# Sliding-window attention scores as 64x64 tiles of the array, in a fused attention, expert and feed-forward kernel

## Chip, cores and metric

One NeuronCore of one Trainium2 chip runs the whole program. The metric is the device time of one execution in microseconds (us); the kernel before took 451.86 us, the median of three runs (451.54, 451.86 and 454.5).

## What is computed

Three blocks in a row, all in float32. Only the first one is changed.

```python
# attention: batch 2, heads 8, sequence 576, head dimension 64
scores = scale * np.matmul(q, k.transpose(0, 1, 3, 2))
rel = pos[:, None] - pos[None, :]
mask = (rel >= 0) & (rel < 64)
scores = np.where(mask, scores, -1000000000.0)
attn = np.exp(scores - max); attn = attn / (sum(attn) + 1e-09)
x = np.matmul(attn, v)            # -> 1152 tokens x 512
# mixture of 8 experts (512 -> 1024 -> 512), each token to its best expert
expert_idx = np.argmax(x @ w_gate, axis=1)
out[i] = gate_w[i] * y[expert_idx[i], pos[i]]
# dense feed-forward 512 -> 2048 -> 512 with h * relu6(h + 3) / 6
```

Each query sees itself and the 63 keys before it, so 64 queries need a window of 128 keys.

## The kernel before

**Tiling.** The 1152 tokens are nine blocks of 128, j = 0 to 8; each block is two groups of 64 queries, g = 2j and 2j + 1 (18 groups). The eight heads are four pairs hp; a pair's two heads lie on partitions 0 to 63 (even head) and 64 to 127 (odd head) after the transposes of q and k.

**A block's steps** are named nodes of a list (lines 659 to 708):

- `lq`, `lk`, `lv` load 128 rows each by DMA from SP's queue; `tq`, `tk`, `tv` (`turn_rows`, L506) transpose them on TensorE (PE), four 128x128 transposes each;
- `eq` (`q_out`, L460 on VectorE or L464 on ScalarE) copies the queries out of PSUM, scaled, into `qd`, a tile of 128 x 4 x 2 x 128. Per pair and group it is block-diagonal: the even head's 64 queries in columns 0 to 63 of partitions 0 to 63, the odd head's in columns 64 to 127 of partitions 64 to 127, and zeros elsewhere. The zeros are written once, by memsets (L376, L377), for the four buffers. So `eq` is two copies of 64 x 512;
- `ek` (L462 or L458) copies the keys into `kT`, `ev` the values into `vT`; `gw`, `ew`, `tw`, `ex` (L541, L555) bring the gate's logits through the same attention, as eight more columns of the values;
- `s` (`scores`, L570) is, per group, one 128x128 matmul per head pair: the block-diagonal queries are the stationary operand, the window of 128 keys of `kT` the moving one. The result has 128 rows, even head's queries above odd head's, in one PSUM bank. There are two banks for scores (0 and 1), taken in turn, one group each;
- `m` (`mask_max`, L583, VectorE) adds the mask and finds the row maximum, four instructions per group; `e` (`exps`, L596, ScalarE) four exponentials; `pt` (L606, PE) four transposes; `ep` (L458 or L462) the copy to `pT`;
- `av` (`values`, L624, PE) is 16 matmuls of 128 x 64 x 73 per block, for the two groups, into alternating column halves of the array; `f` (`finish`, L636 to L652, VectorE) divides and gives logits; `st` stores the rows to `x_dram`.

**What orders them.** `run_nodes` is a list scheduler that runs when the program is built: of the nodes whose needs are met it takes the one with the smallest key (estimated start, a priority from `PRIO`, its cost), and appends its instructions to the queue of PE, VectorE (DVE), ScalarE (ACT), GpSimd (POOL) or SP. For a copy it also chooses the engine, ACT or DVE. Each engine then runs its queue strictly in order. `rings` holds how many buffers of each kind there are; for a node with `take`, a buffer is reserved.

**Routing among the attention.** After five blocks (`f` of j = 4) the logits of 640 tokens are known: `top` (`choose`), `pp`, `pl`, `fl`, `gE`, `ix`, `ie` pick the fullest expert and 128 of its tokens on DVE with small matmuls between; `ga` (POOL, L799) gathers their rows from `x_dram`; `sE` (L460) scales them, and the first products with that expert's weights (`early`) fill PE while the last blocks finish. After `f` of j = 8 come the ranks of the experts (`rk`) and the slots (`sa` to `g0`), then the expert stage, whose weights (64 loads of 512 KB) come from DRAM, and from about 244 us the dense stage.

## Time and profile before

| | |
|---|---|
| median of three runs | 451.86 us |
| the profiled execution's own time | 452.26 us |
| its span, first to last instruction | 450.5 us |
| PE busy | 417.8 us, 93% |
| DVE busy | 323.6 us, 72% |
| ACT busy | 231.4 us, 51% |
| first matmul of scores | 9.54 us |
| last division of the attention (`f` of j = 8) begins | 67.48 us |

The profile is of one execution. The page gives busy times over the whole span; what one stage is limited by is read from windows of it and from timelines, which list instructions in order of their start, with the idle time before one and what ended it in brackets. A matmul's end is modelled and matmuls overlap, so on PE the distance from one start to the next tells what an instruction occupies, not its duration. A float32 matmul is two rows of the trace, a transpose one.

### The profile page before, as it was taken

The numbers are of one execution on the slowest core, as the hardware profiler recorded it, in microseconds if no ns is written. First come the engines' busy times: TensorE is split into PE (matmuls) and PEld (weight loads), VectorE is DVE, ScalarE is ACT, GpSimd is POOL, SyncE is SP. The second block draws the span as 40 slices with busy tenths as digits, with TensorE's granted clock in tenths as the row PEclk, the third lists the DMA queues.
The fourth block names the chain that finished last, engine by engine and source line by source line (L and its number), as shares of the span: only waits on it lengthen the run. The fifth ranks groups of instructions, "written<-read, shape, count | busy, mean of one in ns | idle before, by whom it ended". The sixth has DMA issues, their size and how long they took to land. (4 is left out here: it accounts for less than half of the span.)

```text
span 450.5 us, 8296 instructions
## 1 busy us (share of the span) xinstructions
PE 417.8 (93%) x2911; PEld 358.3 (80%) x2911; DVE 323.6 (72%) x861; ACT 231.4 (51%) x509; POOL 53.3 (12%) x108
## 2 busy tenths in 40 slices
PE   7999898699999899998893999999999999999994
PEld 4889775488788798986693989888888888898993
DVE  1787977679899899989552899999999722322431
ACT  3979863573567976535461744345554222422240
POOL 8624312310002002000000000000000000020011
PEclk9999999999999999999696999999999999999999
DMA  8988884997999899399774134243421000010011
GB/s 144 162 196 191 244 285 147 357 323 248 378 371 355 276 323 308 113 296 336 263 260 155 48 93 113 79 137 95 114 77 44 1 1 0 25 71 0 25 48 47
DMA packets 69651, 75.98 MB, mean 169 GB/s; under 512 B 31105, under 2 KB 49537, under 8 KB 69601
## 3 DMA queue, kind: packets, MB, share of 16 engines
q1 hardware_dynamic: 68016, 70.28, 51.3%
q0 software_dynamic: 1584, 5.08, 3.1%
q8 instruction: 25, 0.41, 0.4%
q14 instruction: 26, 0.20, 0.1%
HBM read 67.49 MB, written 7.86 MB: 167 GB/s over the span
## 5 line engine op out<-in xcount | busy, mean ns | idle before, releaser
L253 PE MATMUL banks<-x,wt 128*128 128x320 f32 (+3 forms) x576 | 108.0, 339 | 7.8 <-DVEq L1878 7.8
L253 PEld LDWEIGHTS banks<-x,wt 128*128 128x128 f32 x576 | 95.8, 191 | 17.5 <-ACT wt L267 8.0
L272 DVE TENSOR_TENSOR wt<-raw,wt 128x512 fp32r<-128x512 f32 x128 | 82.6, 685 | 18.6 <-ACT wt L267 11.3
L253 PE MATMUL banks<-wt,g 128*128 128x512 f32 x384 | 92.8, 390 | 0.0
L267 ACT CAST wt<-raw 128x512 fp32r<-128x512 f32 x128 | 74.9, 622 | 27.0 <-DMA raw<-in_moe_w_dram 14.3
L253 PEld LDWEIGHTS banks<-wt,g 128*128 128x128 f32 x384 | 71.6, 188 | 14.2
L1550 ACT ACTIVATE r<-banks,c_three 128x320 f32<-128x320 f32 (+3 forms) x48 | 27.9, 581 | 70.6 <-PE banks L253 70.6
L1553 DVE SCALAR_TENSOR_TENSOR gf<-r,banks 128x320 f32<-128x320 f32 (+3 forms) x48 | 26.6, 554 | 50.6 <-ACT r L1550 50.3
L253 PE MATMUL banks<-xT,wt 128*128 128x256 f32 (+2 forms) x288 | 40.2, 287 | 3.8 <-ACT wt L267 3.4
L253 PEld LDWEIGHTS banks<-xT,wt 128*128 128x128 f32 x288 | 35.8, 194 | 6.6 <-ACT wt L267 4.5
L253 PE MATMUL banks<-h,wt 128*128 128x256 f32 (+2 forms) x288 | 37.0, 279 | 0.0
L253 PEld LDWEIGHTS banks<-h,wt 128*128 128x128 f32 x288 | 34.6, 192 | 0.5 <-issue 0.5
L1556 ACT CAST g<-gf 128x320 fp32r<-128x320 f32 (+2 forms) x40 | 21.4, 536 | 21.8 <-DVE gf L1553 21.7
L1596 POOL DMA_INDIRECT out_dram<-raw,cidx x4 | 3.9, 982 | 225.0 <-DVE raw L1590 216.8
L1559 DVE TENSOR_TENSOR g<-gf,g 128x320 fp32r<-128x320 f32 (+2 forms) x40 | 23.3, 582 | 8.9 <-ACT g L1556 8.8
L206 ACT ACTIVATE c<-raw 128x512 f32<-128x512 f32 x32 | 21.5, 675 | 13.0 <-DVE t L230 10.4
L253 PE MATMUL banks<-wt,xT 128*128 128x256 f32 x144 | 23.0, 296 | 2.8 <-DVE wt L272 1.6
L253 PEld LDWEIGHTS banks<-wt,xT 128*128 128x128 f32 x144 | 18.9, 189 | 6.6 <-DVE wt L272 3.6
L799 POOL DMA_INDIRECT xg<-x_dram,sidx x10 | 13.9, 1388 | 84.3 <-DVE c L210 38.0
L583 DVE CUSTOM_DVE_ANT_0 neg<-banks,mask 128x128 f32<-128x128 f32 x72 | 16.5, 285 | 10.1 <-PE banks L570 10.1
L596 ACT ACTIVATE pe<-neg,nmx 128x128 f32<-128x128 f32 x72 | 22.8, 393 | 0.7 <-DVE nmx L583 0.5
L253 PE MATMUL banks<-wt,h 128*128 128x512 f32 x72 | 20.6, 423 | 2.1 <-ACT h L1430 2.1
(285 smaller groups left out, 598.9 us busy)
## 6 DMA issues: line engine op xcount, KB each, us to landing
raw<-in_moe_w_dram SPq DMA_DIRECT2D x64, 512.0 KB, 6.7
raw<-in_moe_w_in_dram SPq DMA_DIRECT2D x16, 512.0 KB, 6.0
raw<-in_moe_w_out_dram SPq DMA_DIRECT2D x16, 512.0 KB, 6.1
early<-in_moe_w_dram SPq DMA_DIRECT2D x8, 512.0 KB
wd_dram<-t SPq DMA_DIRECT2D x12, 256.0 KB, 8.1
raw<-wd_dram SPq DMA_DIRECT2D x6, 512.0 KB
x_dram<-xt SPq DMA_DIRECT2D x9, 256.0 KB, 2.4
q_sb<-in_q_dram SPq DMA_DIRECT2D x8, 256.0 KB, 5.3
```

The lines of the kernel that those rows point to most:

```text
L206: nc.scalar.activation(box["c"].bitcast(F32), box["hi"].bitcast(F32), AF.Abs)
L253: nc.tensor.matmul(out, l, r, start=(start and n == 0), stop=(stop and n == len(pairs) - 1))
L267: nc.scalar.copy(hi, r)
L272: V.tensor_tensor(out=lo, in0=r, in1=hi.bitcast(F32), op=ALU.subtract)
L583: V.tensor_tensor_reduce(out=neg[:, hp, :], in0=box["sp", g][:, hp, :], in1=mask[:, g % 2, first, :], scale=-1.0, scalar=3.0e38, op0=ALU.a ...
L596: nc.scalar.activation(pe[:, hp, :], neg[:, hp, :], AF.Exp, bias=nmx[:, hp : hp + 1], scale=-1.0)
L799: nc.gpsimd.indirect_dma_start(out=t, out_offset=None, in_=x_dram[0:n], in_offset=bass.IndirectOffsetOnAxis(ap=index.bitcast(U32), axis=0),)
L1550: nc.scalar.activation(r, ph, AF.Relu, bias=c_three)
L1553: V.scalar_tensor_tensor(out=gf, in0=r, scalar=6.0, in1=ph, op0=ALU.min, op1=ALU.mult)
L1556: nc.scalar.copy(hi, gf)
L1559: V.tensor_tensor(out=lo, in0=gf, in1=hi.bitcast(F32), op=ALU.subtract)
L1596: nc.gpsimd.indirect_dma_start(out=out, out_offset=bass.IndirectOffsetOnAxis(ap=cidx[:, a : a + 1].bitcast(U32), axis=0), in_=o, in_offset ...
```

## The change

Queries are stored without zeros, 128 x 4 x 128, by one copy of 128 x 512, and the eight memsets are gone. One node `s` now computes both groups of a block: for each head pair four products of 64 x 64 x 128, one for each half of the partitions (r: even or odd head) and each group (i). The even heads' results go to one bank, the odd heads' to the other; within a bank, group 2j stands in the upper 64 rows and group 2j + 1 in the lower. So `mask_max` of the first bank (still called g = 2j) now works on all even heads of both groups and that of the second on the odd ones; both need a mask of their own (`tmask`, six GpSimd copies), and `values` picks its rows accordingly. Both banks are one ring entry (`sp`, one buffer), free again when both `mask_max` are done. The scheduler is told new costs, so it makes a new order of the attention.

```diff
+        tmask = ac.tile([128, 3, 128], F32, name="tmask")
+        for i in range(2):
+            r = slice(64 * i, 64 * i + 64)
+            nc.gpsimd.tensor_copy(tmask[r, 0], mask[r, i, 0])
+            nc.gpsimd.tensor_copy(tmask[r, 1], mask[r, i, 1 - i])
+            nc.gpsimd.tensor_copy(tmask[r, 2], mask[r, i, i])
...
-            t = ac.tile([128, H // 2, 2, 128], F32, name=f"qd{i}")
-            eng = nc.gpsimd if i else nc.vector
-            eng.memset(t[0:64, :, :, 64:128], 0.0)
-            eng.memset(t[64:128, :, :, 0:64], 0.0)
-            qd.append(t)
+            qd.append(ac.tile([128, H // 2, 128], F32, name=f"qd{i}"))
...
-                pt, dst = box["tq", j], qd[j % NQD]
-                for s in range(2):
-                    copy(
-                        e, dst[64 * s : 64 * s + 64, :, :, 64 * s : 64 * s + 64],
-                        pt[64 * s : 64 * s + 64].rearrange("p a (n t) -> p a n t", t=64), D ** -0.5,
-                    )
+                copy(e, qd[j % NQD], box["tq", j], D ** -0.5)
...
-        def scores(g):
+        def scores(j):
             def run(e):
-                box["sp", g] = sp = quarters(bank("s"))
-                j, i = divmod(g, 2)
+                box["sp", 2 * j], box["sp", 2 * j + 1] = sp = [quarters(bank("s")) for _ in range(2)]
                 for hp in range(H // 2):
-                    nc.tensor.matmul(
-                        sp[:, hp, :], qd[j % NQD][:, hp, i, :], k_window(hp, g),
-                        start=True, stop=True,
-                    )
+                    for r in range(2):
+                        for i in range(2):
+                            d, t = slice(64 * r, 64 * r + 64), slice(64 * i, 64 * i + 64)
+                            nc.tensor.matmul(
+                                sp[r][t, hp, :], qd[j % NQD][d, hp, t], k_window(hp, 2 * j + i)[d], start=True, stop=True
+                            )
...
-                first = 1 if g % GB == 0 else 0
+                j = g // 2
+                first = [2 * j % GB, (2 * j + 1) % GB].index(0) + 1 if 0 in (2 * j % GB, (2 * j + 1) % GB) else 0
...
-                        out=neg[:, hp, :], in0=box["sp", g][:, hp, :], in1=mask[:, g % 2, first, :], scale=-1.0,
+                        out=neg[:, hp, :], in0=box["sp", g][:, hp, :], in1=tmask[:, first, :], scale=-1.0,
...
-                            box["pT", 2 * j + s][:, h // 2, 64 * (h % 2) : 64 * (h % 2) + 64],
+                            box["pT", 2 * j + h % 2][:, h // 2, 64 * s : 64 * s + 64],
...
-            node(("eq", j), p + PRIO["eq"], {"A": 0.97, "V": 1.2}, q_out(j), [("tq", j)], "qd", [("t", ("tq", j))])
+            node(("eq", j), p + PRIO["eq"], {"A": 0.5, "V": 0.6}, q_out(j), [("tq", j)], "qd", [("t", ("tq", j))])
...
-                node(("s", g), o + PRIO["s"], {"PE": 0.87}, scores(g), needs, "s", [("qd", ("eq", j))] * (g % 2))
-                node(("m", g), o + PRIO["m"], {"V": 0.84}, mask_max(g), [("s", g)], "neg", [("s", ("s", g))])
+                if g % 2 == 0:
+                    needs = [("eq", j), ("ek", j)] + [("ek", j - 1)] * (j > 0)
+                    node(("s", j), o + PRIO["s"], {"PE": 0.93}, scores(j), needs, "sp", [("qd", ("eq", j))])
+                    holders["sp", ("s", j)] = 2
+                node(("m", g), o + PRIO["m"], {"V": 0.84}, mask_max(g), [("s", j)], "neg", [("sp", ("s", j))])
```

The new order differs in the attention alone; from the division of the last block on, every engine's instructions stand as before. Two places of it. First, PE at the start: the queue from the first scores to the second transposes of probabilities (L606 before, L610 after; L570 and L574 are the scores, L541 and L540 the gate's products, L506 and L510 transposes of q, k or v, L555 and L554 the gate's small transpose). Before:

```order
L570 MATMUL banks<-kT,qd_171 128x128 x4
L541 MATMUL banks<-vT,wgb 32x128 x4
L506 MATMUL banks<-ident,q_sb 128x128 x4
L555 MATMUL banks<-ident,vw 128x128
L570 MATMUL banks<-kT,qd_171 128x128 x4
L506 MATMUL banks<-ident,k_sb 128x128 x4
L606 MATMUL banks<-ident,pe 128x128 x4
L506 MATMUL banks<-ident,v_sb 128x128 x4
L570 MATMUL banks<-kT,qd_174 128x128 x4
```

And after:

```order
L574 MATMUL banks<-kT,qd_178 64x128 x16
L540 MATMUL banks<-vT,wgb 32x128 x4
L510 MATMUL banks<-ident,q_sb 128x128 x4
L554 MATMUL banks<-ident,vw 128x128
L510 MATMUL banks<-ident,k_sb 128x128 x4
L610 MATMUL banks<-ident,pe 128x128 x4
L510 MATMUL banks<-ident,v_sb 128x128 x4
L574 MATMUL banks<-kT,qd_179 64x128 x16
L610 MATMUL banks<-ident,pe 128x128 x4
```

The second group's scores no longer stand between the first group's scores and the transposes of its probabilities.

Second, DVE near the end of the attention: the last instruction of the second-to-last `mask_max` (L583, L587), the scaling of the gathered rows (`c`, L460, L464) and the copy of their transposes (`early`). Before, both last `mask_max` stand ahead of the scaling:

```order
L583 ISA neg,nmx<-banks,mask 128x128
L583 ISA nmx 128x1
L460 TENSOR_SCALAR c_1147<-c_1147,sgE 128x512
L458 COPY early<-banks 128x512
L636 TENSOR_SCALAR rd<-banks 128x8
```

After (of the last `mask_max`, the first of its four pairs of rows):

```order
L587 ISA neg,nmx<-banks,tmask 128x128
L587 ISA nmx 128x1
L464 TENSOR_SCALAR c_1188<-c_1188,sgE 128x512
L587 ISA neg,nmx<-banks,tmask 128x128
L587 ISA nmx 128x1
```

The scaling, which waits for the gather's DMA, has moved ahead of the last block's second `mask_max`.

## Rows read from the trace of the kernel before

**Rows 1.** Windows: length, busy (count) of PE, PEld, DVE, ACT, POOL; PE clock, DMA, GB/s
```profile
9.54:42.62 33.08, 33.08 (x411) 29.16 (x412) 25.48 (x128) 27.39 (x80) 14.58 (x42) 1.00 0.89 186
42.62:64.00 21.38, 19.27 (x251) 17.15 (x251) 19.13 (x128) 17.88 (x52) 6.78 (x12) 1.00 0.88 268
64.00:67.48 3.48, 3.35 (x47) 2.70 (x46) 1.97 (x7) 1.08 (x3) 0.00 (x0) 1.00 0.45 172
```

**Rows 2.** Timeline of PE, 20 to 27 us: start, duration, instruction
```profile
20.94 1.06 PE L570 MATMUL banks<-kT,qd 128*128 128x128 f32 x8
21.84 0.60 PE L606 MATMUL banks<-ident,pe 128*128 128x128 f32 x4
...
25.16 0.60 PE L506 MATMUL banks<-ident,v_sb 128*128 128x128 f32 x4
25.60 1.06 PE L570 MATMUL banks<-kT,qd 128*128 128x128 f32 x8
26.58 0.42 PE L541 MATMUL banks<-vT,wgb 128*32 128x128 f32 x8
26.94 0.66 PE L506 MATMUL banks<-ident,q_sb 128*128 128x128 f32 x4
```

**Rows 3.** Timeline of PE: products with the values, two column halves
```profile
23.79 0.23 PE L624 MATMUL banks<-vy,pT 128*64 128x73 f32 x1
23.80 0.23 PE L624 MATMUL banks<-vx,pT 128*64 128x73 f32 x1
23.86 0.23 PE L624 MATMUL banks<-vy,pT 128*64 128x73 f32 x1
```

**Rows 4.** Groups of instructions, 0 to 100 us: copies of queries and others
```profile
L464 ACT ACTIVATE qd<-banks 64x512 f32<-64x512 f32 x14 | 8.3, 592 | 5.9 <-PE banks L506 5.8
L462 ACT COPY pT<-banks 128x512 f32<-128x512 f32 x13 | 7.5, 585 | 3.9 <-PE banks L606 3.7
L458 DVE COPY pT<-banks 128x512 f32<-128x512 f32 x5 | 3.4, 689 | 0.7 <-PE banks L606 0.7
L460 DVE TENSOR_SCALAR qd<-banks 64x512 f32<-64x512 f32 x4 | 2.8, 689 | 0.0
```

**Rows 5.** Timeline of DVE, 42 to 68 us
```profile
42.62 0.17 DVE L636 TENSOR_SCALAR rd<-banks 128x8 f32<-128x8 f32 x1 [0.28 <-PE banks L624]
...
44.09 0.20 DVE L125 TENSOR_REDUCE top_m<-logits 128x5 f32<-128x40 f32 x1
...
55.63 0.28 DVE L583 CUSTOM_DVE_ANT_0 neg<-banks,mask 128x128 f32<-128x128 f32 x1
...
56.47 0.15 DVE L792 CAST eI<-banks 128x1 int32<-128x1 f32 x1
...
56.72 0.16 DVE L794 SCALAR_TENSOR_TENSOR sgE<-banks,sgE 128x1 f32<-128x1 f32 x1
...
62.95 0.48 DVE L460 TENSOR_SCALAR c<-c,sgE 128x512 f32<-128x512 f32 x1 [0.58 <-DMA c<-x_dram,eI]
...
67.48 0.17 DVE L636 TENSOR_SCALAR rd<-banks 128x8 f32<-128x8 f32 x1 [1.26 <-PE banks L624]
```

**Rows 6.** Timeline of ACT, the last two groups' exponentials
```profile
61.56 2.44 ACT L596 ACTIVATE pe<-neg,nmx 128x128 f32<-128x128 f32 x8
```

**Rows 7.** Timelines of the start: DVE, PE, ACT
```profile
1.13 0.48 DVE L376 MEMSET qd<- 64x512 f32 x1
...
2.35 0.27 DVE L660 MEMSET warm<- 128x256 uint32 x1
...
2.67 4.02 PE L663 MATMUL banks<-warm 128*128 128x512 bf16 x9 [2.67 <-DVE warm L660]
6.49 1.06 PE L506 MATMUL banks<-ident,q_sb 128*128 128x128 f32 x4
7.49 1.12 PE L506 MATMUL banks<-ident,k_sb 128*128 128x128 f32 x4
...
7.58 1.20 ACT L464 ACTIVATE qd<-banks 64x512 f32<-64x512 f32 x2 [5.48 <-PE banks L506]
```

More of the change, by code (lines that the diff above doesn't have):

```diff
@@ L398, in tile_kernel @@
         nodes, done, emitted = {}, {}, []
-        rings = {'q': 3, 'k': 4, 'v': 3, 'qd': NQD, 't': 2, 's': 2, 'p': 1, 'o': 1, 'x': 1, 'neg': 4, 'pe': 3, 'pT': 4, 'vT': 3, 'vw': 4, 'xt': 4}
+        rings = {'q': 3, 'k': 4, 'v': 3, 'qd': NQD, 't': 2, 's': 2, 'sp': 1, 'p': 1, 'o': 1, 'x': 1, 'neg': 4, 'pe': 3, 'pT': 4, 'vT': 3, 'vw': 4, 'xt': 4}
         taken = {r: [] for r in rings}
@@ L691, in tile_kernel @@
                 o = p + g % 2
-                needs = [("eq", j), ("ek", j)] + [("ek", j - 1)] * (j > 0)
-                node(("s", g), o + PRIO["s"], {"PE": 0.87}, scores(g), needs, "s", [("qd", ("eq", j))] * (g % 2))
-                node(("m", g), o + PRIO["m"], {"V": 0.84}, mask_max(g), [("s", g)], "neg", [("s", ("s", g))])
+                if g % 2 == 0:
[3 more added lines that the diff above has]
+                node(("m", g), o + PRIO["m"], {"V": 0.84}, mask_max(g), [("s", j)], "neg", [("sp", ("s", j))])
                 node(("e", g), o + PRIO["e"], {"A": 1.17}, exps(g), [("m", g)], "pe", [("neg", ("m", g))])
```

## The prediction

> **What bounds the kernel now.** I read the page first, for where each stage lies, then windows of the attention, then the timelines of PE, DVE and ACT one beside the other, and last the list of what PE and DVE waited for. The windows [rows 1] split the attention in two. From the first scores (9.54 us) to the division of the fifth block (42.62) PE is busy for 33.08 of 33.08 us and no wait of it is listed: PE is the bound, and DVE (25.48) and ACT (27.39) have air. From 42.62 to 64.00 PE has 2.1 us of idle time, and DVE is the dense one: it gets the division of block 4, the choice of the early expert, its flags and its gates (44.09 to 56.88) besides the masks of the last blocks. Between 42.62 and 57.7 the only idle time of DVE is the 0.28 us ahead of the first row [rows 5]. So the second part is bound by DVE, and its end by a gather: the scaling of the gathered rows starts at 62.95, after 0.58 us of waiting for the DMA. The attention ends with the last division at 67.48. Behind it the change leaves every engine's order alone, and the expert stage starts from what that division gives; a shift of 67.48 is a shift of the end. So the question is only how far 67.48 moves.
>
> **Part 1, the scores on PE.** Before, a group's four products occupy 0.90 us from start to start (20.94 to 21.84), 0.98 where the next instruction has another tile shape (25.60 to 26.58) [rows 2]; 18 groups make 16.2 to 17.6 us. After, a block has 16 products of 64x64, each of which streams the same 128 columns as one product of before. Four at a time this costs 0.90 us per block, and with a change of tile shape on both sides about 0.1 more: 1.0 us. Nine blocks make 9.0, so PE loses 7.2 to 8.6 us, about 8. Does the chip run four at a time? The trace shows products side by side in column parts: the two halves for the values start 0.01 us apart and the next pair 0.06 later [rows 3], and the gate's four products, each 128 columns, take 0.36 us together (26.58 to 26.94), where one after another at 0.225 each they would take 0.90 [rows 2]. It shows no product on half of the partitions, so whether the row halves also overlap is open. Bounds: 0.9 us per block (all four together), 1.8 (column pairs together, row halves in turn: no gain), 3.6 (one after another: 16 times 0.225). I take 1.0, since both shapes with column parts overlap, and keep 1.8 and 3.6 for the rivals.
>
> The Trainium skill, "TensorE: Matmul & The Clock Gate" (Part 3, measured speedup), says that products on distinct row groups run at the same time too and gives 3.07 times for four of them. By an estimate from that page, 3.6 / 3.07 makes 1.2 us per block. The skill's "TensorEngine Tiling (Array Packing)" (Key Properties) adds that changing the tiling mode drains the engine; the 0.08 us between 0.90 and 0.98 agrees with a small price of this kind.
>
> **Part 2, the copies of the queries.** A copy of 64 x 512 takes 592 ns on ACT and 689 on DVE; copies of 128 x 512 of another tile take 585 and 689 [rows 4]. So half the partitions cost as much as all, and nine blocks lose nine copies: 18 were 8.3 + 2.8 = 11.1 us, nine are 5.3 to 6.2. But the new order puts six of the nine on DVE (before, two blocks' worth) and three on ACT. With the other copies that changed sides, DVE does 27.1 us ahead of the division of block 4, from 25.48 (the queries +1.4, one group's masks more +0.8, gate copies +1.5, keys and values -2.1); ACT loses about 4.3 in the whole attention. The saving lands on the engine that needs it less.
>
> **Part 3, the start.** The first transposes follow the nine warm-up products, which wait for a memset behind the two query memsets on DVE [rows 7]. Without these the warm-up starts 1.2 us earlier and ends near 5.3; then the transposes wait for the queries' DMA instead, which the trace bounds only by its 3.5 to 5.3 us to landing. The second transposes still start near 7.5 with their own load and need 1.0 us; the copy of the queries is 0.6 shorter, but the keys' copy follows the keys' transposes, not it. I take the first scores 0.2 us earlier, at 9.35. These first transposes take 1.0 us for four, against 0.44 later (25.16 to 25.60 [rows 2]), so PE ran at its lower level, 1.2 GHz, up to there; an earlier warm-up could end that earlier or a pause in it later, so the bounds are 0.8 us earlier and 1.0 later. On GpSimd six mask copies stand where six memsets stood, and nothing waits for them before the first masks at 10.8.
>
> **Part 4, the first half.** Up to the division of block 4 PE had 11 groups of scores; now it has six blocks of them (12 groups), and one more transpose of values: 33.08 - 11 x 0.93 + 6 x 1.0 + 0.44 = 29.3 us, from 9.35 to 38.65. DVE alone, 27.1 us from the first masks at 10.55, would end at 37.7. Two engines that both have work for 27 to 29 us and hand it to each other do not both stay full. I followed the new order row by row with the durations above (masks 0.84 per group, from 55.63 to 56.47 [rows 5]; exponentials 0.305 each, 2.44 for eight [rows 6]) and found four places where PE stands: 0.7 us before the first transposes of probabilities, since the second group's scores no longer cover the masks and exponentials of the first; 0.4 and 0.8 at the gate's products of blocks 4 and 5, whose values ACT copies behind two groups of exponentials; and 0.4 at the values of block 4, behind masks and a copy on DVE. Together 2.3, so the division of block 4 starts at about 40.9, not 42.62: of 3.8 us that PE saved so far, 1.7 arrive. Bounds: 38.9 with no wait at all, 42.6 with twice as much.
>
> **Part 5, the second half.** DVE's chain from there to the end of the early index (before: 42.62 to 56.88, 14.26 us) has the same divisions, choice, flags and gates; it loses a group of masks, a copy of probabilities and three gate copies (2.0 us), gains a copy of keys (0.6), and waits about 0.8 for the values of block 5, whose copy of probabilities stands on ACT behind the exponentials of the choice, a copy of queries and the gate copies. That is 13.6, so the index is there at 54.5. The scaling started 6.07 us after the index (56.88 to 62.95); so it starts at 60.6. Before, both last groups of masks stood ahead of the scaling; now the last one stands behind it, and behind that wait queue the exponentials, transposes and values that the last division needs. Scaling 0.48 and masks 0.84 end at 61.9, exponentials 1.22 later at 63.2, where it was 64.00 [rows 6]. From there to the last division it took 3.48 us (to 67.48), through the transposes, two copies, the early products and the values; with the same tail it begins at 66.6, or 0.3 earlier as PE is emptier. I take 66.3: 1.2 us earlier.
>
> **Sum.** The profiled execution took 452.26 us, its span 450.5 and 1.8 around it. With 1.2 less it is 451.1. It was 0.4 above the median of the runs, so the forecast on the median is 450.7 us. That is no change for a measurement that can tell about 1% (4.5 us): eight us of PE's work go, and one arrives.
>
> **The rivals.**
> *PE's saving arrives nearly whole.* If PE bounded the whole attention, all 8 us would show: 443.9. For it speaks the first window, without a gap. Against it speaks the second: DVE from 42.62 on has no air, and its share of that stretch is hardly smaller after the change. Half-way cases are likelier: no waits in part 4 (2.0 more) and no wait for the gather in part 5 (1.0 more) give 447.7; a shorter way of the gather's DMA adds to that.
> *Row halves in turn.* Then a block costs 1.8 to 2.0 us, what it did before, and the new order, made for short scores, puts the waits on top. Six blocks add 5 to 6 us ahead of the division of block 4, of which the 2.3 us of waits cover some: 44 to 45 in place of 42.62, and the end 2 to 3 later, 454 to 455. One after another at 3.6, six blocks add 15.6 less 2.3, and the last three more: some 465. It decides against the change from about 1.7 us per block, where 6 x 0.7 eats 1.7 plus the 2.3 of cover. Nothing in the trace excludes it, as no product there uses half of the partitions.
> *The pair of banks stalls.* Both banks are now freed together, so the scores of a block wait for two groups of masks, 1.7 us, and those stand behind the flags and gates on DVE (1.7 and 2.1 us). In part 5 this costs nothing, since DVE is the late one; if it also happened in the first half, at two or three blocks, 1 to 2 us more of waiting would bring the division of block 4 back to 42.6 and the end to 452 to 453.
>
> **How the numbers follow.** The forecast, part of PE's saving lost to DVE: 0.58, with a range of its own of 448.5 to 452.5. More of the saving arrives: 0.18, of which 0.15 beyond 1% (below 447.3). Row halves in turn or worse: 0.13, of which 0.10 beyond 1% (above 456.4), as the whole serial case and added waits can reach. Bank stalls: 0.11, with 0.02 beyond. So faster 0.15, slower 0.12, same 0.73. The range from 445 to 456 leaves out the nearly whole saving at one end and the fully serial scores at the other.
>
> **What would show it.** In the profile after: a block of 16 products occupying about 1.0 us from start to start (1.8 or more refutes part 1); the copy of the queries at 0.6 to 0.7 us; gaps on PE between 10 and 41 us, of about 2 us in all, where there were none; the division of block 4 near 40.9; DVE without idle time from there to 54; the scaling of the gathered rows with a longer wait for its DMA, near 1.4 us, and the last masks behind it; the last division near 66.3. If that comes before 63, DVE did not bound the second half and I am wrong; if it comes after 68.5, the scores or the banks are.

## The result and the profile after

The changed kernel took 457.34 us in the median of 12 runs (454.46 to 459.37), the kernel before 451.3 beside it (449.52 to 455.56, 12 runs). The ratio is 1.0104, with a 95% interval from 1.0074 to 1.0134: slower by 1.0%, some 4.7 us, small but clear of the noise. This ratio, and every one below, leaves out the few runs in which the chip was in a slower state, and it is not the quotient of the two medians, which is 1.0134 here. The forecast was 450.7, with a range from 445 to 456.

| profiled execution | before | after | forecast for after |
|---|---|---|---|
| its own time | 452.26 us | 457.3 us | 451.1 us |
| span | 450.5 us | 455.6 us | |
| mean granted clock of PE | 0.983 | 0.968 | |
| scores of a block, start to start | 1.8 to 1.96 us | 1.03 us | 1.0 us |
| division of block 4 | 42.62 us | 44.00 us | 40.9 us |
| scaling of the gathered rows | 62.95 us | 64.90 us | 60.6 us |
| last division | 67.48 us | 73.19 us | 66.3 us |
| ranks of the experts done (`rk`, the cast to `eofI` on DVE) | 71.68 us | 77.39 us | |
| from there to the end of the span | 378.9 us | 378.2 us | |

In these two executions the loss lies wholly in the attention: `rk` comes 5.7 us later, and what follows, in the same order on every engine, takes as long as before. One execution says little about the whole time, though. In twelve of the profiles below the order from the last division on is the same on PE, DVE, ACT and POOL, and they took from 374.9 (E8) to 382.4 us (E6) from `rk` to the end. So the profiles tell where the time of the attention goes, and the ratios over many runs tell what that is worth. The question is how the last division got 5.7 us later while every block's scores became 0.8 to 0.9 us shorter.

The PE timeline of the changed kernel, from the start, an ordinary block, and the end of the attention (start, duration, instruction, and in brackets the idle time before it and what ended it):

```profile
1.41 4.02 PE L667 MATMUL banks<-warm 128*128 128x512 bf16 x9 [1.41 <-DVE warm L664]
6.12 1.08 PE L510 MATMUL banks<-ident,q_sb 128*128 128x128 f32 x4 [0.68 <-DMA q_sb<-in_q_dram]
...
9.54 1.99 PE L574 MATMUL banks<-kT,qd 64*64 64x128 f32 x32
11.46 0.44 PE L540 MATMUL banks<-vT,wgb 128*32 128x128 f32 x4
...
16.01 1.10 PE L574 MATMUL banks<-kT,qd 64*64 64x128 f32 x32
17.04 0.66 PE L610 MATMUL banks<-ident,pe 128*128 128x128 f32 x4
...
61.87 0.66 PE L610 MATMUL banks<-ident,pe 128*128 128x128 f32 x4 [0.29 <-ACT pT L466]
65.44 1.11 PE L820 MATMUL banks<-ident,c 128*128 128x128 f32 x4 [2.91 <-DVE c L464]
66.48 0.38 PE L628 MATMUL banks<-vy,pT 128*64 128x73 f32 x1
...
68.63 1.97 PE L610 MATMUL banks<-ident,pe 128*128 128x128 f32 x8
70.39 1.57 PE L253 MATMUL banks<-early 128*128 128x256 f32 x4
71.89 0.28 PE L628 MATMUL banks<-vy,pT 128*64 128x73 f32 x1
```

A block's 16 products (32 rows, as a float32 matmul is two) occupy 1.03 us from 16.01 to 17.04. That is the whole gain promised on PE. The first block, at 9.54, still runs at half that speed. And near the end PE stands for 2.91 us ahead of L820, the transposes of the gathered rows, which wait for their scaling on DVE. Behind L820 in PE's queue stand the values of block 7 (L628, 66.48 to 68.63), the last transposes of probabilities (68.63) and early products, and then the values of block 8. In the kernel before, the values of block 7 (their last rows at 62.67) are done ahead of these transposes (L814):

```profile
62.67 0.29 PE L624 MATMUL banks<-vx,pT 128*64 128x73 f32 x2
63.49 0.66 PE L814 MATMUL banks<-ident,c 128*128 128x128 f32 x4 [0.53 <-DVE c L460]
```

In the changed kernel everything from 65.44 to 71.48 takes twice what it takes elsewhere: eight transposes occupy 1.76 us here (68.63 to 70.39), where four take 0.44 from start to start in [rows 2] (25.16 to 25.60).

The DVE timeline of the changed kernel, for the same end:

```profile
44.00 0.17 DVE L640 TENSOR_SCALAR rd<-banks 128x8 f32<-128x8 f32 x1 [0.41 <-PE banks L628]
...
57.33 0.16 DVE L800 SCALAR_TENSOR_TENSOR sgE<-banks,sgE 128x1 f32<-128x1 f32 x1
...
62.57 0.08 DVE L587 DVE_READ_ACCUMULATOR2_ANT nmx<- 128x1 f32 x1
64.90 0.49 DVE L464 TENSOR_SCALAR c<-c,sgE 128x512 f32<-128x512 f32 x1 [2.24 <-DMA c<-x_dram,eI]
65.30 0.28 DVE L587 CUSTOM_DVE_ANT_0 neg<-banks,tmask 128x128 f32<-128x128 f32 x1
...
73.19 0.17 DVE L640 TENSOR_SCALAR rd<-banks 128x8 f32<-128x8 f32 x1 [3.01 <-PE banks L628]
```

Before, the scaling waited 0.58 us and both last groups of masks were done by then [rows 5]. Now the index is ready at 57.49 and the scaling starts 7.41 us later (6.07 before), after 2.24 us of waiting, with the last group's masks (65.30) queued behind it although their scores had long been there. ACT shows the same wait one step on; its last four exponentials, which come in [rows 6] without one:

```profile
65.69 1.28 ACT L600 ACTIVATE pe<-neg,nmx 128x128 f32<-128x128 f32 x4 [1.37 <-DVE nmx L587]
```

Windows of the changed kernel (length; busy time and count of PE, PEld, DVE, ACT, POOL; granted clock of PE; DMA share; GB/s), to be held against [rows 1]:

```profile
9.54:44.00 34.46, 32.98 (x520) 25.87 (x520) 26.49 (x142) 24.56 (x73) 13.24 (x22) 1.00 0.89 185
44.00:67.48 23.48, 18.56 (x270) 14.34 (x271) 18.10 (x117) 15.97 (x49) 6.78 (x12) 0.87 0.77 250
67.48:73.19 5.71, 5.71 (x65) 4.96 (x64) 1.37 (x6) 1.17 (x2) 0.00 (x0) 0.65 0.13 50
...
54.42:57.83 3.41, 3.09 (x40) 2.80 (x36) 3.38 (x28) 1.76 (x6) 2.24 (x6) 0.50 1.03 366
60.00:64.66 4.66, 2.24 (x41) 1.56 (x38) 2.07 (x13) 3.57 (x12) 0.00 (x0) 1.00 1.06 374
64.66:71.48 6.82, 6.04 (x47) 5.38 (x48) 3.39 (x15) 2.45 (x6) 0.00 (x0) 0.50 0.35 127
```

This is what the timelines don't say by themselves: from 54.42 to 57.83 and from 64.66 to 71.48 the granted clock is 0.50, which is 1.2 GHz. Ahead of the second fall PE stands from 62.53 us on (the 2.91 us before L820 at 65.44). In the kernel before, the granted clock stays at 1.00 from 8.62 us to 216.84. The trace's record of the clock begins with the first rise (8.62 before, 13.46 after), so a window that begins ahead of it shows 1.00 for that part too, as the first one here does. Up to the rise the lower level is read from the spacing of transposes in the changed kernel: 0.213 us from start to start up to 13.38, and 0.109 from 13.53 on.

The copies of the queries, from the groups of 0 to 100 us, against the first and last of [rows 4]:

```profile
L464 DVE TENSOR_SCALAR qd<-banks 128x512 f32<-128x512 f32 x6 | 4.1, 689 | 0.6 <-ACT pe L600 0.3 <-PE banks L510 0.3
L468 ACT ACTIVATE qd<-banks 128x512 f32<-128x512 f32 x3 | 1.8, 589 | 5.1 <-PE banks L510 5.1
```

Nine copies, 5.9 us, six of them on DVE: as forecast.

### The profile page after: what moved, and what is told of

It is laid out like the page before. It is cut to its first block, busy times and chain, and to the rows that moved or that the text cites. A ratio compares the mean times of both kernels' runs of the same rounds, so it can differ in the third digit from the quotient of the medians.

```text
span 455.6 us, 8576 instructions
## 1 busy us (share of the span) xinstructions
PE 420.7 (92%) x3055; PEld 355.7 (78%) x3055; DVE 322.5 (71%) x860; ACT 226.5 (50%) x499; POOL 50.5 (11%) x108
## 5 line engine op out<-in xcount | busy, mean ns | idle before, releaser
L587 DVE CUSTOM_DVE_ANT_0 neg<-banks,tmask 128x128 f32<-128x128 f32 x72 | 16.3, 286 | 12.1 <-PE banks L574 12.0
L253 PE MATMUL banks<-wt,h 128*128 128x512 f32 x72 | 21.6, 441 | 1.8 <-ACT h L1436 1.8
L230 DVE SCALAR_TENSOR_TENSOR t<-raw,c 128x512 f32<-128x512 uint32 x32 | 22.0, 689 | 0.4
```

What stands on the lines that cost most here:

```text
L230: nc.vector.scalar_tensor_tensor(out=box["t"], in0=box["lo"], scalar=2.0 ** -52, in1=box["c"].bitcast(F32), op0=ALU.mult, op1=ALU.mult)
L253: nc.tensor.matmul(out, l, r, start=(start and n == 0), stop=(stop and n == len(pairs) - 1))
L587: V.tensor_tensor_reduce(out=neg[:, hp, :], in0=box["sp", g][:, hp, :], in1=tmask[:, first, :], scale=-1.0, scalar=3.0e38, op0=ALU.add, op ...
```

## The experiments

Two theories stood after this reading, and one doubt on each. *Order*: the new plan assumes that the gathered rows are there 3.0 us after the gather's issue, for which it counts 1.04 us on GpSimd; the trace shows 6.0 us from the start of the issue to the landing before and 7.3 after. With the shorter scores the plan puts the scaling ahead of the last masks (DVE) and L820 ahead of the values of block 7 (PE), and the end of the attention waits for a DMA. *Start*: the warm-up products begin earlier (1.41 us, 2.67 in [rows 7]), end earlier, and PE pauses at 5.4 to 6.1 us; the granted clock is full only from 13.46 us on. The doubts: is it the queue or the clock that costs, and is it the tiles themselves?

The table holds all kernels. "Clock" is the mean granted clock over the kernel's runs; times of the profile are of its one profiled execution: division of block 4 (f4), start of the scaling, last division (f8), `rk`.

| | edit | median us | ratio, interval | clock | f4 | scaling | f8 | rk |
|---|---|---|---|---|---|---|---|---|
| before | | 451.3 to 452.5 | 1 | 0.980 | 42.62 | 62.95 | 67.48 | 71.68 |
| after | the change | 457.34 | 1.0104 [1.0074, 1.0134] | 0.966 | 44.00 | 64.90 | 73.19 | 77.39 |
| E1 | after, longer warm-up | 456.0 | 1.0082 [1.0049, 1.0116] | 0.968 | 41.92 | 62.67 | 68.16 | 72.36 |
| E2 | after, scaling later | 452.6 | 1.0022 [0.9979, 1.0065] | 0.972 | 43.38 | 64.16 | 68.69 | 72.89 |
| E3 | E1 and E2 | 451.9 | 1.0003 [0.9968, 1.0038] | 0.976 | 42.37 | 63.56 | 68.09 | 72.30 |
| E4 | before, earlier warm-up | 452.39 | 0.9975 [0.9933, 1.0017] | 0.980 | 42.76 | 64.02 | 68.54 | 72.75 |
| E5 | E3, gathered rows last on PE | 453.28 | 1.0035 [1.0001, 1.0068] | 0.976 | 41.86 | 62.72 | 66.37 | 70.53 |
| E6 | E3, early loads held | 453.17 | 1.0009 [0.9974, 1.0045] | 0.976 | 42.29 | 61.20 | 66.00 | 70.21 |
| E7 | E3, queries on ACT alone | 453.1 | 1.0032 [1.0001, 1.0064] | 0.971 | 43.80 | 64.98 | 69.21 | 73.36 |
| E8 | E3, PE kept busy | 451.04 | 0.9993 [0.9967, 1.0019] | 0.981 | 42.02 | 62.75 | 67.27 | 71.48 |
| E9 | after, the wait filled | 454.92 | 1.0105 [1.0048, 1.0162] | 0.972 | 43.42 | 64.60 | 70.39 | 74.59 |
| E10 | after, order on PE alone | 454.48 | 1.0104 [1.0041, 1.0168] | 0.973 | 42.61 | 64.06 | 69.82 | 74.03 |
| E11 | before, scaling ahead of the last masks | 454.31 | 1.0078 [1.0029, 1.0127] | 0.978 | 42.54 | 63.74 | 70.13 | 74.34 |
| E12 | E8 and E6 | 451.08 | 1.0006 [0.9972, 1.0040] | 0.979 | 42.08 | 62.61 | 67.13 | 71.34 |

**E1, the start.**

```diff
-    NWARM = 9
+    NWARM = 12
```

> The changed kernel with 12 warm-up products in place of 9, so that PE has no pause before the first transposes of queries. Theory S (start): the pause of 0.68 us at 5.4 us, which the earlier warm-up opened, delays the rise of PE's clock from 8.6 us (kernel before) to 13.5; without the pause the rise comes near 9, the first division comes at about 18.7 instead of 20.55, and the time falls by 1.5 to 2 us against the changed kernel. Theory G (gather): the start doesn't matter, as DVE's chain and the gather set the end; within 0.5 us of the changed kernel. Theory W (waits between the engines in the new order): within 0.5 us too, with the first waits unchanged.

In the profiled execution the clock was full from 4.65 us to 52.44, the division of block 4 came 2.1 us earlier (41.92), and the last one 5 us earlier. Its order at the end is that of the changed kernel, but DVE waited only 0.68 us for the gather and PE 1.46 us ahead of L820, the clock was full there, and the tail from the scaling to the last division took 5.49 us instead of 8.29. But over ten runs the ratio is 1.0082, hardly below 1.0104, and the profiled execution (453.78) was the fastest of them. So the start is worth some 0.2%, which the two intervals don't tell from nothing; one profile alone would have misled here.

**E2, the order of the gather.** Only the time that the planner assumes for the gather changes; what moves in the program is the scaling (behind the last masks on DVE) and L820 (behind the values of block 7 on PE).

```diff
-        node("ga", p + PRIO["ga"], {"P": 1.04}, early_gather, ["ie"], lag=3.0)
+        node("ga", p + PRIO["ga"], {"P": 1.04}, early_gather, ["ie"], lag=3.8)
```

> The changed kernel with the scheduler told 3.8 us in place of 3.0 for the early gather; on the engines this moves only two things: the scaling of the gathered rows behind the last masks on DVE, and the transposes of these rows behind the values of block 7 on PE. Theory G: the last masks no longer wait 2.2 us for the gather's DMA, PE's idle stretch of 2.9 us shrinks, and with it the half clock from 64.7 to 71.5 us; the last division comes at about 69.5 instead of 73.2, the time falls by 3 to 4 us. Theory S: no change (under 0.5 us). Theory W: no change, the transposes of the rows still hold PE up (under 1 us).

DVE timeline of E2:

```profile
56.78 0.16 DVE L800 SCALAR_TENSOR_TENSOR sgE<-banks,sgE 128x1 f32<-128x1 f32 x1
...
62.90 0.28 DVE L587 CUSTOM_DVE_ANT_0 neg<-banks,tmask 128x128 f32<-128x128 f32 x1
...
64.16 0.49 DVE L464 TENSOR_SCALAR c<-c,sgE 128x512 f32<-128x512 f32 x1 [0.34 <-DMA c<-x_dram,eI]
...
68.69 0.17 DVE L640 TENSOR_SCALAR rd<-banks 128x8 f32<-128x8 f32 x1 [1.26 <-PE banks L628]
```

The last masks now begin at 62.90, ahead of the scaling; the gather takes as long as in the changed kernel (7.2 us from the index's end), but the last division comes 4.53 us behind the scaling instead of 8.29. The ratio falls from 1.0104 to 1.0022, and the two intervals don't meet: this one move holds most of the loss.

**E3, both.** The edits of E1 and E2 together.

> Both edits at once. Theory S and G together: 5 to 6 us less than the changed kernel, 451 to 452, that is, equal to the kernel before. If only one holds, its part alone. Theory W: within 1 us of the changed kernel.

Ratio 1.0003, where E1, with the same start and the early scaling, has 1.0082: the move is worth 0.8% a second time, and the tiles, with the loss mended, are worth nothing that can be measured. The division of block 4 is at 42.37 and the last at 68.09 (67.48 before).

**E4, the start alone in the kernel before.** The query memsets of DVE go to GpSimd, so the warm-up starts as early as in the changed kernel.

```diff
-            eng = nc.gpsimd if i else nc.vector
+            eng = nc.gpsimd
```

> The kernel before with the two query memsets of DVE moved to GpSimd, so that the warm-up starts 1.2 us earlier as in the changed kernel, and nothing else changed. Theory S: a pause before the first transposes, the clock rises at about 13 us instead of 8.6, 2 us more ahead of the division of block 4, and 1 to 2 us more in the whole. Rival: the start is hidden, or a little better: -0.3 to 0.

The clock was full only from 10.12 us on, 1.5 us later than before, and the time did not change (0.9975, interval from 0.9933 to 1.0017). An early warm-up does shift the clock's rise, but costs the whole nothing that shows.

**E5 to E8, on E3: what still holds the end.** E5 moves L820 behind the last transposes of probabilities, E6 holds the last five of the eight early expert loads until the gather is issued, so that three stand ahead of it instead of six, E7 takes the queries' copies off DVE, E8 puts six dummy matmuls ahead of the scores of blocks 6 to 8.

E5:

```diff
-        node("tE", p + PRIO["turn"], {"PE": 0.44}, early_turn, ["sE"], "x")
+        node("tE", p + PRIO["turn"], {"PE": 0.44}, early_turn, ["sE", ("pt", NG - 1)], "x")
```

> The kernel of e3 with the transposes of the gathered rows behind the last two groups' transposes of probabilities on PE (they now need them; the early products move behind the last values, and the fill work of the expert stage is planned anew). Theory G2: in e3 PE's queue still stands at the gather (2 us of idle time ahead of 64.1), and the last probabilities behind it; without that the last division comes 2 to 3 us earlier, near 65.5, and the time is 1 to 2.5 us below e3. Rival: the early products, now later, are missed by the stage behind, and the gain is given back: within 0.7 us of e3.

E6:

```diff
-                node(("wl", u, h), p + 2 * u + h, {"D": 1.46}, early_load(u, h), ["pl"], lag=2.0)
+                node(("wl", u, h), p + 2 * u + h, {"D": 1.46}, early_load(u, h), ["pl"] + ["ga"] * (2 * u + h >= 3), lag=2.0)
```

> The kernel of e3 with five of the eight early weight loads (512 KB each) issued behind the gather instead of ahead of it; the other engines' order is the same. Theory D (contention): the gather took 6.2 us from the index to the scaling in the kernel before and 7.4 to 7.8 in the changed kernel, because six loads are now issued in one go ahead of it; with only three ahead it takes 6 us or less, the scaling comes 1.5 us earlier and the time falls by 1 to 1.5 us. Rival: the DMA queues aren't what it waits for; still 7.5 us, and the late weights cost up to 1 us.

E7:

```diff
-            node(("eq", j), p + PRIO["eq"], {"A": 0.5, "V": 0.6}, q_out(j), [("tq", j)], "qd", [("t", ("tq", j))])
+            node(("eq", j), p + PRIO["eq"], {"A": 0.5}, q_out(j), [("tq", j)], "qd", [("t", ("tq", j))])
```

> The kernel of e3 with all nine copies of queries on ACT (the scheduler may not choose DVE for them), which makes a new order of the attention. Theory V (DVE is the bound of the second half and the partner of PE in the first): DVE loses six copies, 3.7 us; the division of block 4 comes 1 us earlier or more, and the time falls by 1 to 2 us. Rival: ACT, which holds the exponentials, becomes the late one: no change or up to 2 us more.

E8:

```diff
+                if j >= 6:
+                    for _ in range(6):
+                        nc.tensor.matmul(banks[:, 5, 128:512], warm[:, 0:128], warm[:, 0:384], start=True, stop=True)
```

> The kernel of e3 with six extra products of zeros (128x384, bf16) on PE ahead of the scores of blocks 6, 7 and 8, whose results are not used, 18 products, 3 us of PE's time, in a stretch where PE waits for DVE. Theory C (clock): in all profiles of the changed kernel's kind PE's clock was halved for 3.4 to 6.8 us at 52 to 58 us, after gaps of PE that the kernel before doesn't have; with PE kept busy it stays at its upper level there, and the last division comes 0.5 to 1.5 us earlier, the time 0.5 to 1.5 us lower. Rival: PE isn't what is late there; the clock stays up and the time is equal, or 0.5 to 2 us higher by the extra products.

DVE timeline of E6, index and scaling:

```profile
55.65 0.16 DVE L800 SCALAR_TENSOR_TENSOR sgE<-banks,sgE 128x1 f32<-128x1 f32 x1
...
61.20 0.48 DVE L464 TENSOR_SCALAR c<-c,sgE 128x512 f32<-128x512 f32 x1
```

From start to start 5.55 us, without a wait, against 7.57 in the changed kernel. The gather itself is read from the list of DMA issues (45 to 70 us; the last number is the time in us from issue to landing), first in E3, then in E6:

```profile
c<-x_dram,eI POOLq DMA_INDIRECT x1, 7.6
c<-x_dram,eI POOLq DMA_INDIRECT x1, 4.5
```

It is 6.0 in the kernel before, 7.3 in the changed one, 6.5 in E8, and 3.5 in E12, which holds the same loads as E6. E6 has E3's order on PE, DVE, ACT and POOL, so the gather was slow because of the loads issued ahead of it, with which it shares the DMA engines (374 GB/s from 60.00 to 64.66 in the windows of the changed kernel). The kernel before issues six as well, but three from 48.65 and three from 53.97 us; the new order issues them in one go, from 52.06 to 55.38.

E5 and E6 both bring the attention's end 1.1 to 1.5 us ahead of the kernel before, and their ratios, 1.0035 and 1.0009, show nothing of it. In their one profile each it takes 381.8 and 382.4 us from `rk` to the end instead of 378.9. E5 has another order there; E6 has E3's (376.7 us in its profile), and E12, with the same held loads, took 377.7. So for E6 no loss in the later stages is shown beyond one execution, and its interval, from 0.9974 to 1.0045, is as wide as the lead. E7 speaks against DVE's copies of the queries as what holds the first half: without them the division of block 4 came later (43.80, in a profile with half the clock from 14.98 to 18.39 us). E8 kept the clock full through the attention (it first fell at 234 us) and was the best of the changed kernels, at 451.04, but its interval, from 0.9967 to 1.0019, holds 1.

**E9 to E11, clock, queue or tiles.** E9 puts dummy matmuls into PE's wait ahead of L820 (in `early_turn`, L816); no other instruction moves.

```diff
+            for _ in range(18):
+                nc.tensor.matmul(banks[:, 5, 128:512], warm[:, 0:128], warm[:, 0:384], start=True, stop=True)
```

> The changed kernel with 18 dummy matmuls (bf16, 128 x 128 x 384, into a PSUM bank nobody reads) ahead of the transposes of the gathered rows on PE, and nothing else, so PE works through most of the 2.9 us in which it stood for these rows, and the queues keep their order. Theory clock: the tail is long because the granted clock fell to half at 64.66 to 71.48 us after that pause; it now stays full there and the last division begins 2 to 2.5 us earlier (70.7 to 71.2 instead of 73.19), the ratio to the kernel before is near 1.005. Theory queue: what costs is the wait itself, with the values of block 7 and the last transposes behind it; the last division stays within 0.7 us of 73.2 whatever the clock, and the ratio stays near 1.010.

PE timeline of E9, and the window that has half the clock in the changed kernel:

```profile
62.57 3.09 PE L819 MATMUL banks<-warm 128*128 128x384 bf16 x18
65.50 0.60 PE L822 MATMUL banks<-ident,c 128*128 128x128 f32 x4
67.21 1.09 PE L610 MATMUL banks<-ident,pe 128*128 128x128 f32 x8
68.14 1.03 PE L253 MATMUL banks<-early 128*128 128x256 f32 x4
```

```profile
64.66:71.48 6.82, 6.82 (x93) 5.67 (x91) 4.28 (x20) 2.70 (x8) 0.00 (x0) 1.00 0.38 137
```

With the wait filled the clock stays at 1.00, and the same work, from the gathered rows' transposes to the values of block 8, takes 3.59 us (65.50 to 69.09) instead of 6.45 (65.44 to 71.89). The last division comes 5.79 us behind the scaling, against 8.29. So in the profile some 2.5 of the 5.7 us are the clock's, and the last division, at 70.39, came a little before what the clock theory named (0.6 us of it by an earlier division of block 4). The whole time is not resolved: four runs, 1.0105 with an interval that reaches from 1.0048 to 1.0162 and so holds both theories' values.

E10 changes the order on PE alone:

```diff
-        node("tE", p + PRIO["turn"], {"PE": 0.44}, early_turn, ["sE"], "x")
+        node("tE", p + PRIO["turn"], {"PE": 0.44}, early_turn, ["sE", ("av", NJ - 2)], "x")
```

> The changed kernel with one more need for the transposes of the gathered rows: the values of block 7 come ahead of them on PE; on DVE the scaling still stands ahead of the last two masks. If PE's queue is what costs (values of block 7 and the last transposes stand behind the gathered rows), the last division moves from 73.19 to about 70.5 or earlier and the ratio falls to near 1.003, as the later gather gave. If DVE's queue is what costs (the last masks, and with them the last exponentials, stand behind the scaling), only the 1.1 us of the values of block 7 are saved: last division about 72, ratio near 1.008.

PE timeline of E10:

```profile
64.60 1.11 PE L820 MATMUL banks<-ident,c 128*128 128x128 f32 x4 [1.88 <-DVE c L464]
65.51 1.92 PE L610 MATMUL banks<-ident,pe 128*128 128x128 f32 x8
67.21 1.38 PE L253 MATMUL banks<-early 128*128 128x256 f32 x4
```

The values of block 7 are gone from behind L820, and the last division comes at 69.82. But 1.4 of these 3.4 us are the start of this execution (division of block 4 at 42.61 instead of 44.00); from there on 2.0 us are saved, between what the two theories named. The clock is at half again behind the 1.88 us wait, and the ratio did not fall (1.0104). E2 is E10 with one more difference, the scaling behind the last masks on DVE: there it takes 25.3 us from the division of block 4 to the last one, 27.2 in E10, and the ratio is 1.0022. That speaks for DVE's queue as the larger part; with four runs the two intervals still overlap, and it stays open. (For E9 and E10 the quotients of the medians, 1.0073 and 1.0064 against 451.61, lie below the ratios given, one more reason to leave both open.)

E11 is the control: the scaling ahead of the last masks, in the kernel before, whose scores are whole matmuls. On DVE that is the changed kernel's order. On PE it is another: the values of block 7 stay ahead of L814, and two groups of early products come between the last two groups of transposes.

```diff
-        node("ga", p + PRIO["ga"], {"P": 1.04}, early_gather, ["ie"], lag=3.0)
+        node("ga", p + PRIO["ga"], {"P": 1.04}, early_gather, ["ie"], lag=2.6)
```

> The kernel before with the planner's assumed time of the gather cut from 3.0 to 2.6 us, so that the scaling of the gathered rows comes ahead of the last masks on DVE and the early products ahead of the last transposes on PE; the arithmetic is the same. Theory order: this alone costs the kernel before what it costs the changed one: last division 2 to 5 us later than 67.48, ratio 1.004 to 1.010. Rival tiles: the loss belongs to the 64x64 tiles or to the clock under them, and the order is harmless where the scores are full matmuls: last division within 1 us, ratio within 1.002.

DVE timeline of E11:

```profile
57.22 0.16 DVE L794 SCALAR_TENSOR_TENSOR sgE<-banks,sgE 128x1 f32<-128x1 f32 x1
...
60.67 0.28 DVE L583 CUSTOM_DVE_ANT_0 neg<-banks,mask 128x128 f32<-128x128 f32 x1
...
63.74 0.49 DVE L460 TENSOR_SCALAR c<-c,sgE 128x512 f32<-128x512 f32 x1 [1.72 <-DMA c<-x_dram,eI]
64.14 0.28 DVE L583 CUSTOM_DVE_ANT_0 neg<-banks,mask 128x128 f32<-128x128 f32 x1
...
70.13 0.17 DVE L636 TENSOR_SCALAR rd<-banks 128x8 f32<-128x8 f32 x1 [3.72 <-PE banks L624]
```

PE timeline of E11:

```profile
64.28 0.66 PE L814 MATMUL banks<-ident,c 128*128 128x128 f32 x4 [0.84 <-DVE c L460]
64.78 0.60 PE L606 MATMUL banks<-ident,pe 128*128 128x128 f32 x4
65.61 1.99 PE L253 MATMUL banks<-early 128*128 128x256 f32 x8 [0.24 <-ACT early L462]
67.44 0.60 PE L606 MATMUL banks<-ident,pe 128*128 128x128 f32 x4
```

On DVE the same picture as in the changed kernel: 1.72 us of waiting, masks behind it; the last division is 2.65 us late, with the clock full from 7.29 us to 218.91. The ratio is 1.0078, with an interval clear of 1. So an order of this kind alone, without any of the new tiles and without a fall of the clock in the attention, costs what it was said to cost; that the loss needs the tiles is refuted. How it divides between the two queues is not shown by E11.

**E12, the best parts together.** E8's dummy matmuls and E6's held loads.

> The changed kernel with the longer warm-up, the later scaling, six dummy matmuls ahead of the scores of blocks 6, 7 and 8, and the last five early loads held until the gather is issued. If the two gains add, the last division begins near 65.5 us (66.0 with the loads held, 67.3 with PE kept busy) and the ratio is 0.995 to 0.998. If later stages take the gain back, as with the loads held alone, the ratio is 0.999 to 1.002.

The two gains did not add: last division at 67.13, ratio 1.0006. The gather lands 3.5 us after its issue, at 59.8, but the scaling starts at 62.61 without a wait for it: so what stands ahead of it in DVE's queue, and no longer the gather, is late (the index is ready at 56.24, and at 55.81 in E6). No version was found that beats the kernel before.

**The clock over all runs.** Each run lists its mean granted clock. In 81 runs of the kernel before, beside the experiments, it lies between 0.969 and 0.992, and the time goes with it: the fitted line is 246 us per 1.0, so 2.5 us for each 0.01, with a correlation of -0.74. That is an association within one kernel (within the runs of E1 the line is 46 us per 1.0, within those of E6 366). It does not say which of the two brings the other, as a PE that waits longer for a DMA would both take longer and be granted less; and using it for another kernel is an estimate. By it the changed kernel, whose clock is lower by 0.0133 in the mean, loses 3.3 us, and 1.6 of its 4.9 us (mean of its runs against the mean of the 81) are left. Done the same way against the runs of before in their own group, the kernels with the early scaling have 0.5 (E1), 1.6 (E9), 1.5 (E10) and 2.3 us (E11) left, and those with the late one have -0.9 (E2), -0.7 (E3), -0.1 (E5), -0.9 (E6), -0.7 (E7), -0.9 (E8) and -0.2 (E12). Each has a standard error of 0.4 to 0.7 us, so E1 alone can't be told from the late ones; the groups as a whole lie about 2 us apart. By this estimate, then, about 2 us are the order's at an equal clock, and up to 3 the clock's, and at an equal clock and in the right order the tiles come out some 0.6 us ahead. The mean clock is 0.971 to 0.976 in E2, E3 and E5 to E7, 0.980 in the kernel before, and 0.981 where E8 kept PE busy. That a PE with less to do is granted less, and that this takes the 0.6 us back, is argued from these means and not shown: E8's ratio can't be told from E3's.

## Why the prediction was wrong

The forecast for the last division was 66.3 us in the profile, and it came at 73.19. The 6.9 us between are, step by step:

| step | forecast | measured | difference |
|---|---|---|---|
| start (part 3), by E1 against after: 44.00 - 41.92 | 0 | 2.1 | +2.1 |
| first half (part 4), division of block 4 in E1 | 40.9 | 41.92 | +1.0 |
| DVE's chain to the index's end (part 5) | 13.6 | 13.49 | -0.1 |
| index's end to the scaling | 6.07 | 7.41 | +1.3 |
| scaling to the last division | 5.7 | 8.29 | +2.6 |

**Part 1, right.** A block occupies 1.03 us (1.0 forecast). Row halves and column halves do run together, and the rival of row halves in turn (1.8) fell. The Trainium skill's "TensorE: Matmul & The Clock Gate" (Part 3, measured speedup), with 3.07 times for four products on row groups of 32, would by estimate have made it 1.2; here it is 16 x 0.225 / 1.03 = 3.5 times, and the measurement decides.

**Part 2, right.** 589 and 689 ns, six on DVE.

**Part 3, wrong in its middle, beyond its bounds in this execution.** The first scores stayed at 9.54 (9.35 forecast, inside the bounds), but they and all up to 13.46 us ran at half the clock, which costs more than the 1.0 us allowed. Kernels with the same start had the division of block 4 at 44.00, 43.38, 43.42 and 42.61 (after, E2, E9, E10): the profiled execution of the changed kernel was the worst of four, and over many runs the start is worth little (E1, E4).

**Part 4, the mechanism right, the sum too small.** The waits stand where the new order was followed to them: at the gate's products and at the transposes of probabilities. PE's waits in E1 between 8 and 42 us (engine, line, what it waited for: total, times, longest):

```profile
PE banks L510 <- ACT kT L466: 0.7, 1, 0.7
PE banks L540 <- ACT vT L466: 0.7, 1, 0.7
PE banks L610 <- ACT pe L600: 0.6, 1, 0.6
PE banks L610 <- ACT pT L466: 0.2, 1, 0.2
```

Without the first, which is ahead of the scores, these are 1.5 us; 2.3 were forecast. But from the first scores of E1 (9.12) to its division of block 4 it took 32.80 us, and as long (32.80 or 32.81) in E3, E5, E6, E8 and E12; 31.55 were forecast, and 33.08 was the time before. The term that was too small is PE's own work, 29.3 us: 32.80 less 1.5 of waits leaves 31.3 that are not. Part of the 2.0 us is the change of tile shape. The sum counts it once per block of scores, at 0.1 us; it costs 0.09 us each time, on the way into the scores and on the way out of them. From its start to the next one, a transpose's row takes 0.203 us where another tile shape follows and 0.109 where the same does, so that four transposes occupy 0.53 us ahead of the scores in E1 (24.13 to 24.66), and 0.44 before [rows 2]. From the first scores to the division of block 4 the rows of the traces have 21 changes in the kernel before and 32 in E1, 1.0 us more; the sum holds 0.3 of it (6 x 0.1 added, 11 x 0.03 taken off). The rest was not taken apart.

```profile
24.13 0.60 PE L510 MATMUL banks<-ident,v_sb 128*128 128x128 f32 x4
24.66 1.10 PE L574 MATMUL banks<-kT,qd 64*64 64x128 f32 x32
```

Of the 8 us to be saved in the whole attention, 0.3 arrive at this point.

**Part 5, where the prediction failed.** The chain on DVE came out to a tenth. What failed is the step behind it: "the scaling started 6.07 us after the index" and "with the same tail". The text saw that the last masks would stand behind the scaling and priced that wait at about 1.4 us; it took the gather's length of before for a gather that now runs beside six loads issued in one go (7.41 us to the scaling, landing 7.3 us after the issue, against 6.0 before and 4.5 in E6, with the loads held). It did not follow the second queue: on PE, L820 stands ahead of the values of block 7, so the wait on DVE becomes a wait of 2.91 us on PE with a block's values behind it. And it took the tail at the clock of before, where a PE that had waited was granted half. At a full clock the tail is what was forecast, in the same order of both queues: 5.79 us in E9 and 5.49 in E1, against 5.7. So of the 2.6 us by which the tail was mis-sized the clock is nearly all, in this execution. Over many runs it is the order that decides: the forecast took it as given, at 1.2 us more than the 4.53 of before, and E2, which undoes it, falls to 1.0022. The Trainium skill's "TensorE: Matmul & The Clock Gate" (Part 1, HAM oscillation) describes a kernel whose array falls back to the lower clock in its waits for a DMA and starts the next burst at it; the windows of the changed kernel agree, with the fall at 64.66.

**The rivals.** That PE's saving arrives whole, or half of it, fell: nothing that can be measured arrives even in E3. The pair of banks cost 0.24 us at one place (54.23 us, `s` of block 7, behind the masks) and DVE's chain to the index came out as forecast all the same. The slower outcome came by none of the rivals named: the early index had been read as a thing that sets the end by its time, not by its place in two queues.

What stays open: how the 4.7 us divide between clock and queue in the whole time (the profiles say about 2.5 and 3, the fitted line 3.3 and 1.6), how the order's part divides between DVE's queue and PE's (E10 against E2), and whether the earlier end of the attention in E5 and E6 is worth anything in the whole.

## What to carry to other kernels

When a change shortens one step, a list scheduler moves others: look in the new order for any instruction that waits for a DMA and now stands ahead of work on the last path, on every engine's queue, and price it with the transfer's measured time under the load that the new order puts beside it. An engine that has had work taken away has more pauses, and its granted clock may take back what was saved; so read the mean granted clock beside every time. And a mended version (here 3.8 in place of 3.0 us for the gather) belongs beside a change before the change itself is judged: the tiles cost nothing that could be measured, the order did.

## What had not been expected of the hardware

With the same instructions at the start, the clock was full from 13.46, 4.94, 4.52 and 9.89 us on in four profiles (after, E2, E9, E10; in E2 and E9 it fell once more at about 8 us). So a difference of 1.4 us in the first half can come from one execution alone.

A gather of 128 rows of 2 KB landed from 3.5 us (E12) and 4.5 us (E6) to 7.6 us (E3) after its issue, with the loads issued ahead of it being the difference between E3 and E6; the price of such a DMA is not a constant of the kernel.

A change of tile shape on PE cost 0.09 us each time (0.203 us for a row in place of 0.109), so tiles that are mixed with other shapes pay twice per block, 0.18 us beside the 0.90 that the products take.
